# One load queue with the input first, and token-major denominators in the linear-attention layers of a four-layer kernel

## The chip, the cores and the metric

The kernel runs on one core of a Trainium2 chip. The metric is the device time of one execution in microseconds (us), as a median over several executions. A core has five engines that run side by side and wait for one another through semaphores: TensorE (PE in the profile, with its weight loads listed apart as PEld), VectorE (DVE), ScalarE (ACT), GpSimd (POOL) and SyncE (SP), which here only issues transfers. TensorE's clock is granted by a throttle; "granted clock 0.5" means half speed.

## The reference

The input is one sequence of 2048 tokens with 512 channels in bf16. Four layers follow one another, A, B, A, B. Both kinds have 32 heads of 16 channels. The two A layers share their weights, and so do the two B layers.

```python
def A(x, wqkv, wo):                  # linear attention
    q, k, v = split(x @ wqkv)        # each (32 heads, 2048, 16)
    phi = lambda t: where(t > 0, t + 1, exp(t)) + 1e-6
    pq, pk = phi(q), phi(k)
    kv  = einsum("bhsd,bhse->bhde", pk, v)
    z   = einsum("bhsd->bhd", pk)
    num = einsum("bhqd,bhde->bhqe", pq, kv)
    den = einsum("bhqd,bhd->bhq", pq, z)[..., None] + 1e-6
    return merge(num / den) @ wo

def B(x, wqkv, wo): ...              # softmax attention, sliding window of 256

x = x + A(layernorm(x), A_wqkv, A_wo)
x = x + B(layernorm(x), B_wqkv, B_wo)
x = x + A(layernorm(x), A_wqkv, A_wo)
x = x + B(layernorm(x), B_wqkv, B_wo)
```

What matters here is that `den` is one number for each token and head: 2048 x 32 numbers, a sixteenth of `num`.

## The kernel before

The kernel is a chain of stages: setup, and then for each layer the projection to q, k and v (qkv), the attention, and the output projection. Each stage is a block with one instruction list for each engine, and at the end of a block all engines meet. Time saved by one engine in a stage therefore counts only if that engine was what the stage's end waited for.

**Setup.** Three engines issue loads, each on its own queue. GpSimd builds constants, VectorE builds masks out of them and only then takes the statistics of x. ScalarE makes the layernorm's factor (`rstd`) as exp(-0.5 ln(var + eps)).

```python
# SyncE                               # T = 16 tiles of 128 tokens
for gi in range(4):
    load(xres[:, 4 tiles of group gi], x)        # 512 KB each
load(wA_o); load(wB_o)
# ScalarE
load(wA_qkv)                                     # 1536 KB
wait(statistics); ln_rstd = Exp(-0.5 * Ln(var + eps))
# GpSimd
load(wB_nat)                                     # 1536 KB
memset(...); iota(...)
g.drain()
affine_select(ident ...); affine_select(maskLo ...); affine_select(maskHi ...)
signal(constants)
# VectorE
wait(constants)
... masks out of the constants ...
for gi in range(4):
    wait(x group gi)
    for t in group gi: bn_stats(ln_stats[:, t], xres[:, t])
for t in range(T): bn_aggr(ln_mv[:, t], ln_stats[:, t])
signal(statistics)
```

**A-attention.** Numerator and denominator are both made channel-major, that is, with channels on the partitions and tokens along the free dimension. The denominator is made as a full 128x512 tile, in which each of a head's 16 partitions holds the same number. `KV8` is the K-V product masked to blocks of 16x16, and `Z8` is z spread over the same blocks. The division is a Ln and an Exp on ScalarE and a multiply on VectorE. TensorE's results go to PSUM tensors; a slot is a part of one, which the kernel lets TensorE overwrite only after it has been read.

```python
# TensorE
for f in range(4): pkv[f] = sum over 16 tiles of pk[t].T @ vA[t]   # 64 matmuls
for u in range(16):                       # u = (f, c): 128 channels, 512 tokens
    if u >= 2: wait(Ln u - 2)             # two PSUM slots
    pe.matmul(pden[:, u % 2, :], Z8[:, f, :], pqT[:, f, c])        # 128x512
for u in range(16):
    if u >= 2: wait(multiply u - 2)       # two PSUM slots
    pe.matmul(pnum[:, u % 2, :], KV8[:, f, :], pqT[:, f, c])
# ScalarE
for u in range(16): d2[:, u] = Ln(pden[:, u % 2] + 1e-6)
a.drain()
for u in range(16): d2[:, u] = Exp(-d2[:, u])
# VectorE
for u in range(16):
    wait(Exp u); wait(matmul u)
    v.tensor_tensor(oT[:, f, c], pnum[:, u % 2, :], d2[:, u, :], mult)
```

**Output projection.** For A, `oT` is channel-major already and is used as it is. For B, the result is token-major, and each tile takes four transposes on TensorE and a copy on ScalarE first:

```python
def emit_matmuls(pe, t):
    for f in range(4):
        lhsT = oTt[:, t % 2, f, :] if from_tok else oT[:, f, tile t]
        pe.matmul(pwo[:, t % 4, :], lhsT, w_o[:, f, :], start=(f == 0), stop=(f == 3))
```

VectorE then adds the residual and takes the next layernorm's statistics.

The softmax here doesn't subtract the row's maximum and nothing guards it: scores larger than these inputs give would overflow.

## Time and profile before

The time is 866.53 us, the median of 4 runs (865.32 to 867.28). I cut the profiled execution (865.6 us) into stages, each from the first TensorE matmul of a stage to the first of the next:

| stage | us |
|---|---|
| setup | 29.50 |
| layer 1 (A): qkv, attention, projection | 66.76, 29.56, 27.30 |
| layer 2 (B) | 297.32 |
| layer 3 (A): qkv, attention, projection | 65.75, 30.43, 26.91 |
| layer 4 (B) | 292.07 |

The B layers are two thirds of the time, and the change doesn't touch them. It touches setup, the two A-attentions and the two A-projections.

The following lines are from the timeline of the kernel before, in setup. The columns are start in us, duration in us, engine, source line, operation, output and input, shapes, count; in brackets stands how long the engine had been idle and what released it.

```profile
13.62 0.29 POOL L200 TENSOR_SCALAR_AFFINE_SELECT ident<-ident 128x128 bf16<-128x128 bf16 x1 [10.30 <-issue]
14.54 0.15 DVE L219 TENSOR_SCALAR itmp_m<-itmp_p 128x1 int32<-128x1 int32 x1 [14.54 <-POOLq L213]
15.78 9.59 DVE L231 BATCH_NORM_STATS2 ln_stats<-xres 128x6 f32<-128x512 bf16 x16
25.44 1.17 DVE L234 BATCH_NORM_AGGREGATE ln_mv<-ln_stats 128x2 f32<-128x6 f32 x16
26.67 0.31 ACT L151 ACTIVATE ln_rstd<-ln_mv,epsln 128x16 f32<-128x16 f32 x1 [24.05 <-DVEq L235]
27.03 1.28 ACT L153 ACT_TABLE_LOAD   x1
29.50 1.01 PE L329 MATMUL pst<-ident,xn 128*128 128x128 bf16 x8 [29.50 <-DVE xn L427]
```

It is a serial chain. GpSimd stands idle for 10.30 us and goes on at 13.62; VectorE starts its masks at 14.54, its statistics at 15.78; ScalarE follows at 26.67, and TensorE gets its first work at 29.50. The next lines are the page's list of DMA issues of the kernel before: output and input, queue, count, KB each, and the median us from issue to landing.

```profile
xres<-in_A_x_dram SPq DMA_DIRECT2D x4, 512.0 KB, 13.5
wA_qkv<-in_A_wqkv_dram ACTq DMA_DIRECT2D x1, 1536.0 KB, 12.3
wB_nat<-in_B_wqkv_dram POOLq DMA_DIRECT2D x1, 1536.0 KB, 12.1
```

The three queues carry data at the same time. Both weights have landed by 13.4 us (0.80 + 12.3 = 13.1 for A, 1.32 + 12.1 = 13.4 for B), but of the input, which is needed first, only one quarter: its four landings are recorded at 8.55, 14.33, 15.85 and 17.35 us. GpSimd's own load landed at 13.4 us, just ahead of the end of GpSimd's idle time.

The timeline of the kernel before, in the first A-attention, with the same columns:

```profile
101.92 9.90 ACT L572 ACTIVATE d<-pden,eps 128x512 f32<-128x512 f32 x16 [4.43 <-remote]
111.90 1.28 ACT L575 ACT_TABLE_LOAD   x1
113.19 9.90 ACT L575 ACTIVATE d<-d,zero 128x512 f32<-128x512 f32 x16
113.94 1.30 DVE L562 TENSOR_TENSOR oT<-pnum,d 128x512 bf16<-128x512 f32 x2 [11.52 <-ACT d L575]
115.41 1.30 DVE L562 TENSOR_TENSOR oT<-pnum,d 128x512 bf16<-128x512 f32 x2 [0.16 <-PE pnum L533]
```

ScalarE works for 9.90 + 1.28 + 9.90 = 21.1 us. VectorE can't start its multiplies before the first Exp, so it waits 11.52 us; from then on two multiplies take 1.47 us (113.94 to 115.41), with a short wait for TensorE after each pair. The same stage in the view by groups (line, engine, operation, names, shapes, count; busy us, mean ns of one; idle us before it and its releasers), and the view by windows of the multiply loop (window, its length, then busy us and instruction count of PE, PEld, DVE, ACT and POOL, granted clock, DMA share, GB/s):

```profile
L562 DVE TENSOR_TENSOR oT<-pnum,d 128x512 bf16<-128x512 f32 x16 | 10.4, 691 | 12.7 <-ACT d L575 11.7 <-PE pnum L533 1.0
```

```profile
114.00:125.50 11.50, 8.51 (x14) 1.47 (x14) 10.35 (x16) 9.10 (x15) 0.00 (x0) 0.50 0.00 0
```

The loop ran at a granted clock of 0.50, with VectorE busy for 10.35 of 11.50 us.

### The profile page before, as it was taken

How to read it: one execution, taken by the hardware profiler on the slowest of the kernel's cores; microseconds unless marked ns; L12 is line 12 of the kernel's file. 1: busy time of each engine (PE TensorE's matmuls, PEld its weight loads, DVE VectorE, ACT ScalarE, POOL GpSimd, SP SyncE). 2: the span in 40 equal slices, each digit the busy share in tenths (PEclk: the TensorE clock that was granted, in tenths of full speed). 3: DMA queues.
4: the chain of work that ended last, by engine and by line, in shares of the span. 5: the costliest groups of instructions: out<-in, count | busy, mean ns of one | idle time of the engine just before them, and what ended most of it. 6: DMA issues, size and time to landing. Idle time of an engine off the chain costs nothing. (4 is left out here: it accounts for less than half of the span.)

```text
span 865.6 us, 16040 instructions
## 1 busy us (share of the span) xinstructions
PE 678.7 (78%) x5478; PEld 316.6 (37%) x5504; DVE 594.0 (69%) x2750; ACT 632.4 (73%) x884; POOL 5.7 (1%) x22
## 2 busy tenths in 40 slices
PE   0578675798888888888867887848978888888888
PEld 0333412443343343434433342323433434333344
DVE  3577658434777878777685783854378787887875
ACT  0577670456999999999656778134589999999984
POOL 1000000000000000000000000000000000000000
PEclk9999958799555555555688996769965555555559
DMA  8000000000000000000000000000000000000002
GB/s 291 0 1 1 1 0 0 2 1 1 1 2 2 1 2 1 2 1 2 2 1 1 1 1 0 1 0 1 1 1 2 2 2 2 1 2 2 2 2 98
DMA packets 6353, 9.41 MB, mean 11 GB/s; under 512 B 384, under 2 KB 5504, under 8 KB 6272
## 3 DMA queue, kind: packets, MB, share of 16 engines
q1 hardware_dynamic: 5472, 5.24, 1.9%
q10 hardware_dynamic: 528, 1.57, 0.5%
q0 software_dynamic: 272, 1.57, 0.5%
q8 instruction: 44, 0.72, 0.3%
q14 instruction: 37, 0.30, 0.1%
HBM read 6.29 MB, written 2.10 MB: 10 GB/s over the span
## 5 line engine op out<-in xcount | busy, mean ns | idle before, releaser
L786 ACT ACTIVATE PTs<-st,zero 128x768 bf16<-128x768 f32 (+2 forms) x512 | 404.8, 859 | 22.0 <-PE st L741 10.2
L823 DVE TENSOR_TENSOR PTs<-PTs,maskHi 128x128 bf16<-128x128 bf16 x1024 | 220.2, 221 | 79.2 <-ACT PTs L786 78.2
L760 PE MATMUL U<-vB,PTs 128*128 128x17 bf16 x2880 | 163.1, 179 | 67.3 <-DVE PTs L827 62.6
L760 PEld LDWEIGHTS U<-vB,PTs 128*128 128x128 bf16 x2880 | 116.2, 106 | 244.4 <-DVE PTs L827 228.4
L827 DVE TENSOR_TENSOR PTs<-PTs,maskLo 128x128 bf16<-128x128 bf16 x896 | 196.2, 219 | 0.0
L741 PE MATMUL st<-qT,kT 16*128 16x384 bf16 (+2 forms) x512 | 121.5, 472 | 2.2 <-PEq L311 2.2
L741 PE MATMUL st<-qT,kTB 32*128 32x384 bf16 (+2 forms) x512 | 122.5, 474 | 0.0
L329 PE MATMUL pst<-ident,xn 128*128 128x128 bf16 x256 | 30.0, 270 | 82.4 <-DVE xn L427 78.2
L367 PE MATMUL pss<-wA_qkv,xnT 128*128 128x512 bf16 x255 | 64.0, 395 | 0.3 <-issue 0.2
L367 PE MATMUL pss<-xnT,wB_qk 128*128 128x512 bf16 x248 | 61.5, 391 | 0.8 <-ACT xnT L389 0.4
L656 DVE TENSOR_TENSOR xres<-pwo,xres 128x512 bf16<-128x512 f32 x64 | 43.5, 680 | 21.6 <-PE pwo L621 21.6
L389 ACT ACTIVATE xnT<-pst 128x512 bf16<-128x512 bf16 x64 | 34.9, 595 | 30.1 <-PE pst L329 29.6
L242 ACT ACTIVATE tmpE<-pss,zero 128x512 f32<-128x512 f32 x64 | 44.0, 688 | 17.5 <-PE pss L367 11.0
L461 DVE TENSOR_SCALAR kTB<-kT,maskB 128x512 bf16<-128x512 bf16 x32 | 11.3, 353 | 64.9 <-ACT kT L408 64.9
L151 ACT ACTIVATE ln_rstd<-ln_mv,epsln 128x16 f32<-128x16 f32 x4 | 1.2, 308 | 73.5 <-DVEq L666 49.4
L329 PEld LDWEIGHTS pst<-ident,xn 128*128 128x128 bf16 x256 | 19.6, 116 | 95.4 <-DVE xn L427 51.6
L246 DVE TENSOR_SCALAR tmpE<-tmpE 128x512 f32<-128x512 f32 x64 | 27.0, 422 | 25.6 <-ACT tmpR L243 25.3
L803 DVE TENSOR_TENSOR o_tok<-U,densb 128x128 bf16<-128x128 f32 x128 | 37.4, 292 | 9.6
L243 ACT ACTIVATE tmpR<-pss,zero 128x512 bf16<-128x512 f32 x64 | 43.9, 686 | 0.0
L408 ACT ACTIVATE qT<-pss 128x512 bf16<-128x512 f32 x32 | 19.1, 597 | 32.7 <-PE pss L367 32.7
L367 PEld LDWEIGHTS pss<-wA_qkv,xnT 128*128 128x128 bf16 x256 | 26.3, 103 | 34.7 <-issue 7.9
L562 DVE TENSOR_TENSOR oT<-pnum,d 128x512 bf16<-128x512 f32 x32 | 20.9, 690 | 26.2 <-ACT d L575 24.0
(69 smaller groups left out, 648.6 us busy)
## 6 DMA issues: line engine op xcount, KB each, us to landing
xres<-in_A_x_dram SPq DMA_DIRECT2D x4, 512.0 KB, 13.5
out_dram<-xres SPq DMA_DIRECT2D x16, 128.0 KB, 1.7
wA_qkv<-in_A_wqkv_dram ACTq DMA_DIRECT2D x1, 1536.0 KB, 12.3
wB_nat<-in_B_wqkv_dram POOLq DMA_DIRECT2D x1, 1536.0 KB, 12.1
wA_o<-in_A_wo_dram SPq DMA_DIRECT2D x1, 512.0 KB, 13.8
wB_o<-in_B_wo_dram SPq DMA_DIRECT2D x1, 512.0 KB, 9.4
```

The source lines that it names most:

```text
L242: a.activation(self.tmpE[:, js, :], ps_ap, ACT.Exp, bias=z)
L243: return a.activation(self.tmpR[:, js, :], ps_ap, ACT.Relu, bias=z)
L329: mm = pe.transpose(pst[sl2][:, kt, :], self.xn[:, sl2, kt * P : (kt + 1) * P], self.ident[:])
L367: mm = pe.matmul(pss[:, sl, :], lhsT, rhs, start=(kt == 0), stop=(kt == 3))
L389: s_cp.inc(a.activation(self.xnT[:, :, t * P : (t + 1) * P], pst[sl2][:], ACT.Copy))
L656: s_res.inc(v.tensor_tensor(self.xres[:, t, :], pwo[:, sl, :], self.xres[:, t, :], ALU.add))
L741: mm = pe.matmul(ST[sl][:, e, 0:n], lhsT, rhs, start=True, stop=True, tile_position=(32 * (hs % 4), 0))
L760: mm = pe.matmul(ut[:, hs, 0:17], lhsT, rhs, start=(ci == 0), stop=(ci == len(cl) - 1))
L786: a.activation(self.PTs[:, j % NJS, hp[0] : hp[0] + 2, 0:n], ST[sl][:, :, 0:n], ACT.Exp, bias=self.zero1[:], scale=DH ** -0.5,)
L803: v.tensor_tensor(self.o_tok[:, jd, fd * P : (fd + 1) * P].rearrange("p (h d) -> p h d", d=DH), ut[:, :, 0:DH], dsb.to_broadcast([P, 8, DH ...
L823: op = v.tensor_tensor(self.PTs[:, js, hs, 0:P], self.PTs[:, js, hs, 0:P], self.maskHi[:], ALU.mult)
L827: op = v.tensor_tensor(self.PTs[:, js, hs, 2 * P : 3 * P], self.PTs[:, js, hs, 2 * P : 3 * P], self.maskLo[:], ALU.mult,)
```

## The change

The intent has two parts. In setup, all loads go onto SyncE's queue with x in front, and the statistics come ahead of the masks, so that VectorE starts as soon as x is there. In A-attention, the denominator is made token-major, that is, with tokens on the partitions, as 32 numbers for each token rather than 512. Its reciprocal then costs a sixteenth of the elements, and the multiply reads it broadcast over the 16 channels of a head. The price is that the result is token-major, so A's projection needs the transposes that B's has.

```diff
 # setup, SyncE
   for gi in range(NG): load(xres group gi)
+  s_wA.inc(e.dma_start(self.wA_qkv[:], ...), 16)
+  s_wB.inc(e.dma_start(self.wB_nat[:], ...), 16)
   load(wA_o); load(wB_o)
 # setup, ScalarE
-  s_wA.inc(a.dma_start(self.wA_qkv[:], ...), 16)
 # setup, GpSimd
-  s_wB.inc(g.dma_start(self.wB_nat[:], ...), 16)
 # setup, VectorE
+  for gi in range(NG): wait(x group gi); bn_stats of its four tiles
+  bn_aggr of 16 tiles
+  v.wait_ge(s_c.h, s_c.v(1)); s_stat.inc(v.nop())
   v.wait_ge(s_c.h, s_c.v(1))
   ... masks, and bm8 [P, 8] ...
-  bn_stats and bn_aggr as above
@@ A-attention @@
 # TensorE
-  16 x pe.matmul(pden[:, sl, :], self.Z8[:, f, :], pqT of 512 tokens)
-  16 x pe.matmul(pnum[:, sl, :], self.KV8[:, f, :], pqT of 512 tokens)
+  for t in range(T):
+      for f in range(4):
+          pe.matmul((pdA if t < KD else pdB)[:, t, f * 8 : (f + 1) * 8],
+                    self.pqT[:, f, t * P : (t + 1) * P], self.Zs[:, f, :])
+  for t in range(T):
+      if t >= 2: pe.wait_ge(s_od.h, s_od.v(t - 1))
+      for f in range(4):
+          pe.matmul(pnum[:, t % 2, f * P : (f + 1) * P],
+                    self.pqT[:, f, t * P : (t + 1) * P], self.KV8[:, f, :])
 # VectorE                                                  KD = 4
-  16 x v.tensor_tensor(oT[...], pnum[:, sl, :], self.d2[:, u, :], ALU.mult)
+  for t in range(KD): v.reciprocal(self.den_all[:, t, :], pdA[:, t, :])
+  for t in range(T):
+      if t == KD: v.wait_ge(s_r.h, s_r.v(1))
+      v.tensor_tensor(o_tok[:, t, :], pnum[:, t % 2, :],
+                      self.den_all[:, t, :].unsqueeze(2).to_broadcast([P, H, DH]), ALU.mult)
 # ScalarE
-  16 x Ln of 128x512, then 16 x Exp of 128x512
+  a.activation(rest, pdB[:, KD:T, :], ACT.Ln, bias=self.eps6[:])        # 128x384
+  s_r.inc(a.activation(rest, rest, ACT.Exp, bias=self.zero1[:], scale=-1.0))
@@ A's projection @@
-  self.phase_wo(self.wA_o, last=last, first=(li == 0), from_tok=False)
+  self.phase_wo(self.wA_o, last=last, first=(li == 0), from_tok=True)
```

Buffers, PSUM tiles and semaphores that follow from this are cut. VectorE's reciprocals leave out the 1e-6 that the Ln adds as its bias.

More of the change, by code (lines that the diff above doesn't have):

```diff
@@ L91, in run @@
             self.blockmask = self.sb("blockmask", [P, P], dt.float32)
+            self.bm8 = self.sb("bm8", [P, 8], dt.float32)
             self.maskLo = self.sb("maskLo", [P, P], dt.bfloat16)
@@ L102, in run @@
             self.itmp_t = self.sb("itmp_t", [P, P], dt.int32)
+            self.itmp_t8 = self.sb("itmp_t8", [P, 8], dt.int32)
+            self.itmp_m8 = self.sb("itmp_m8", [P, 8], dt.int32)
             self.ln_stats = self.sb("ln_stats", [P, T, 6], dt.float32)
@@ L115, in run @@
                         self.vA = self.lsb(lctx, "vA", [P, T, 4, 132], dt.bfloat16)
-                        self.oT = self.lsb(lctx, "oT", [P, 4, self.S], dt.bfloat16)
+                        self.o_tok = self.lsb(lctx, "o_tokA", [P, T, D], dt.bfloat16)
+                        self.oTt = self.lsb(lctx, "oTtA", [P, 2, 4, P], dt.bfloat16)
                         self.KV8 = self.lsb(lctx, "KV8", [P, 4, P], dt.bfloat16)
-                        self.Z8 = self.lsb(lctx, "Z8", [P, 4, P], dt.bfloat16)
+                        self.Zs = self.lsb(lctx, "Zs", [P, 4, 8], dt.bfloat16)
                         self.zc = self.lsb(lctx, "zc", [P, 4], dt.float32)
@@ L121, in run @@
                         self.tmpR = self.lsb(lctx, "tmpR", [P, 2, 512], dt.bfloat16)
-                        self.d2 = self.lsb(lctx, "d2", [P, 4 * C, 512], dt.float32)
+                        self.den_all = self.lsb(lctx, "den_all", [P, T, H], dt.float32)
                         self.phase_qkv("A", first=(li == 0))
                         self.phase_attn_A(first=(li == 0))
-                        self.phase_wo(self.wA_o, last=last, first=(li == 0), from_tok=False)
+                        self.phase_wo(self.wA_o, last=last, first=(li == 0), from_tok=True)
                 else:
@@ L177, in _ @@
                     s_xg[gi].inc(e.dma_start(self.xres[:, gi * tg : (gi + 1) * tg, :], xv[:, gi * tg : (gi + 1) * tg, :]), 16)
+                s_wA.inc(e.dma_start(self.wA_qkv[:], self.A_wqkv.rearrange("(kt p) c -> p kt c", p=P)), 16)
+                s_wB.inc(e.dma_start(self.wB_nat[:], self.B_wqkv.rearrange("(kt p) c -> p kt c", p=P)), 16)
                 s_wAo.inc(e.dma_start(self.wA_o[:], self.A_wo.rearrange("(kt p) c -> p kt c", p=P)), 16)
@@ L182, in _ @@
             def _(a):
-                s_wA.inc(a.dma_start(self.wA_qkv[:], self.A_wqkv.rearrange("(kt p) c -> p kt c", p=P)), 16)
                 a.wait_ge(s_stat.h, s_stat.v(1))
@@ L188, in _ @@
             def _(g):
-                s_wB.inc(g.dma_start(self.wB_nat[:], self.B_wqkv.rearrange("(kt p) c -> p kt c", p=P)), 16)
                 g.memset(self.ident[:], 0.0)
@@ L198, in _ @@
                 g.iota(self.itmp_t[:], pattern=[[1, P]], base=0, channel_multiplier=0)
+                g.iota(self.itmp_t8[:], pattern=[[1, 8]], base=0, channel_multiplier=0)
                 g.drain()
@@ L217, in _ @@
             def _(v):
+                for gi in range(NG):
+                    v.wait_ge(s_xg[gi].h, s_xg[gi].v16(1))
+                    for t in range(gi * tg, (gi + 1) * tg):
+                        v.bn_stats(self.ln_stats[:, t, :], self.xres[:, t, :])
+                v.drain()
+                for t in range(T):
+                    v.bn_aggr(self.ln_mv[:, t, :], self.ln_stats[:, t, :])
+                v.drain()
+                v.wait_ge(s_c.h, s_c.v(1))
+                s_stat.inc(v.nop())
                 v.wait_ge(s_c.h, s_c.v(1))
@@ L226, in _ @@
                 v.drain()
-                s_c.inc(v.tensor_single_scalar(self.blockmask[:], self.itmp_m2[:], 0.0, ALU.is_equal), 1)
-                for gi in range(NG):
-                    v.wait_ge(s_xg[gi].h, s_xg[gi].v16(1))
-                    for t in range(gi * tg, (gi + 1) * tg):
-                        v.bn_stats(self.ln_stats[:, t, :], self.xres[:, t, :])
+                v.tensor_single_scalar(self.blockmask[:], self.itmp_m2[:], 0.0, ALU.is_equal)
+                v.tensor_tensor(self.itmp_m8[:], self.itmp_p[:, 0:8], self.itmp_t8[:], ALU.subtract)
                 v.drain()
-                for t in range(T):
-                    v.bn_aggr(self.ln_mv[:, t, :], self.ln_stats[:, t, :])
-                v.drain()
-                s_stat.inc(v.nop())
+                s_c.inc(v.tensor_single_scalar(self.bm8[:], self.itmp_m8[:], 0.0, ALU.is_equal), 1)
         self.commit_all()
@@ L488, in phase_attn_A @@
         s_kvz = self.sem("kvz")
-        s_nd = self.sem("nd")
-        s_ln2 = self.sem("lnden")
-        s_d2 = self.sem("d2")
+        s_den = self.sem("den")
+        s_dcp = self.sem("dcp")
+        s_r = self.sem("rall")
+        s_num = self.sem("num")
         s_od = self.sem("odone")
-        s_num = self.sem("num")
         s_wB = self.sem("ld_wB")
         s_pm = self.sem("permB")
-        NU = 4 * C
         with (
@@ L499, in phase_attn_A @@
             nc.psum_tensor(self.uname("pnum"), [P, 2, 512], dt.float32) as pnum,
-            nc.psum_tensor(self.uname("pden"), [P, 2, 512], dt.float32) as pden,
+            nc.psum_tensor(self.uname("pden"), [P, 16, H], dt.float32) as pdA,
+            nc.psum_tensor(self.uname("pden"), [P, 16, H], dt.float32) as pdB,
             nc.Block() as blk,
         ):
+            KD = 4
             @blk.tensor
@@ L516, in _ @@
                     s_kv.inc(mm)
-                for f in range(4):
-                    pe.wait_ge(s_kvz.h, s_kvz.v(f + 1))
-                    for c in range(C):
-                        u = f * C + c
-                        sl = u % 2
-                        if u >= 2:
-                            pe.wait_ge(s_ln2.h, s_ln2.v(u - 1))
-                        rhs = self.pqT[:, f, c * 512 : (c + 1) * 512]
-                        s_nd.inc(pe.matmul(pden[:, sl, :], self.Z8[:, f, :], rhs, start=True, stop=True))
-                for f in range(4):
-                    for c in range(C):
-                        u = f * C + c
-                        sl = u % 2
-                        if u >= 2:
-                            pe.wait_ge(s_od.h, s_od.v(u - 1))
-                        rhs = self.pqT[:, f, c * 512 : (c + 1) * 512]
-                        s_num.inc(pe.matmul(pnum[:, sl, :], self.KV8[:, f, :], rhs, start=True, stop=True))
+                pe.wait_ge(s_kvz.h, s_kvz.v(4))
+                for t in range(T):
+                    sl = t % 2
+                    mm = None
+                    for f in range(4):
+                        mm = pe.matmul(
+                            (pdA if t < KD else pdB)[:, t, f * 8 : (f + 1) * 8],
+                            self.pqT[:, f, t * P : (t + 1) * P],
+                            self.Zs[:, f, :],
+                            start=True,
+                            stop=True,
+                        )
+                    s_den.inc(mm)
+                for t in range(T):
+                    sl = t % 2
+                    if t >= 2:
+                        pe.wait_ge(s_od.h, s_od.v(t - 1))
+                    mm = None
+                    for f in range(4):
+                        mm = pe.matmul(
+                            pnum[:, sl, f * P : (f + 1) * P],
+                            self.pqT[:, f, t * P : (t + 1) * P],
+                            self.KV8[:, f, :],
+                            start=True,
+                            stop=True,
+                        )
+                    s_num.inc(mm)
             @blk.vector
@@ L538, in _ @@
                     v.wait_ge(s_wB.h, s_wB.emitted)
-                    last = None
+                    lastop = None
                     for qk in range(2):
@@ L545, in _ @@
                                 i_ap = self.wB_nat[:, kt, c0 : c0 + 128].rearrange("p (eh el d) -> p el eh d", eh=2, el=4, d=DH)
-                                last = v.tensor_copy(o_ap, i_ap)
-                    s_pm.inc(last)
+                                lastop = v.tensor_copy(o_ap, i_ap)
+                    s_pm.inc(lastop)
                 for f in range(4):
@@ L552, in _ @@
                     v.drain()
-                    s_kvz.inc(
-                        v.tensor_scalar(self.Z8[:, f, :], self.blockmask[:], self.zc[:, f : f + 1], None, op0=ALU.mult)
-                    )
-                for u in range(NU):
-                    f, c = u // C, u % C
-                    sl = u % 2
-                    v.wait_ge(s_d2.h, s_d2.v(u + 1))
-                    v.wait_ge(s_num.h, s_num.v(u + 1))
+                    s_kvz.inc(v.tensor_scalar(self.Zs[:, f, :], self.bm8[:], self.zc[:, f : f + 1], None, op0=ALU.mult))
+                v.wait_ge(s_den.h, s_den.v(KD))
+                for t in range(KD):
+                    v.reciprocal(self.den_all[:, t, :], pdA[:, t, :])
+                v.drain()
+                for t in range(T):
+                    sl = t % 2
+                    if t == KD:
+                        v.wait_ge(s_r.h, s_r.v(1))
+                    v.wait_ge(s_num.h, s_num.v(t + 1))
                     s_od.inc(
                         v.tensor_tensor(
-                            self.oT[:, f, c * 512 : (c + 1) * 512], pnum[:, sl, :], self.d2[:, u, :], ALU.mult
+                            self.o_tok[:, t, :].rearrange("p (h e) -> p h e", e=DH),
+                            pnum[:, sl, :].rearrange("p (h e) -> p h e", e=DH),
+                            self.den_all[:, t, :].unsqueeze(2).to_broadcast([P, H, DH]),
+                            ALU.mult,
                         )
@@ L568, in _ @@
             def _(a):
-                for u in range(NU):
-                    sl = u % 2
-                    a.wait_ge(s_nd.h, s_nd.v(u + 1))
-                    s_ln2.inc(a.activation(self.d2[:, u, :], pden[:, sl, :], ACT.Ln, bias=self.eps6[:]))
+                rest = self.den_all[:, KD:T, :]
+                a.wait_ge(s_den.h, s_den.v(T))
+                a.activation(rest, pdB[:, KD:T, :], ACT.Ln, bias=self.eps6[:])
                 a.drain()
-                for u in range(NU):
-                    s_d2.inc(a.activation(self.d2[:, u, :], self.d2[:, u, :], ACT.Exp, bias=self.zero1[:], scale=-1.0))
+                s_r.inc(a.activation(rest, rest, ACT.Exp, bias=self.zero1[:], scale=-1.0))
         self.commit_all()
```

## The prediction

> **What bounds the kernel now.** Busy time per stretch shows four layers: two linear-attention (A), two sliding-window (B). In B (210 to 422, 632 to 847 us) ScalarE is 96% busy, untouched by the change. It touches three serial stretches:
>
> - Setup. The timeline puts the first matrix work (transposes) at 29.5 us. VectorE starts at 14.54 us, released by GpSimd, idle until 13.62 us (its own load lands 12.1 us after issue). Then masks 1.2 us, sixteen bn_stats 9.6 us, aggregation 1.2 us, ScalarE's rstd with a 1.28 us table load 1.95 us.
> - A-attention, 96.2 to 125.5 us, and 516.2 to 546.2 us. K-V product 5.4 us; then 16 Ln of a 128x512 denominator 9.9 us, a table load 1.28 us, 16 Exp 9.9 us; VectorE's 16 multiplies start behind the first Exp, 0.73 us each, alternating with two PSUM slots at a granted clock of 0.5.
> - A output projection: 21.8 us from first matmul to last bn_stats, paced by VectorE at 1.19 us a tile.
>
> **What changes.**
>
> *Setup.* All loads go onto one queue, x first; bn_stats precede the masks. The Trainium skill, "DMA: Bandwidth & Descriptors", Queues, rings and completion order, says each DMA engine round-robins between queues with work; the trace agrees: three queues moved about 400 GB/s together and x landed a median 13.5 us after issue. Alone, at 350 GB/s or better (the single-queue end of the load, 14 to 18 us), the first 512 KB should land at about 5 us and the rest ahead of VectorE. bn_stats run 5 to 14.7, aggregation to 15.9, rstd to 18; masks hide behind ScalarE. First transposes about 18.5 us: 10.8 us saved, all critical. Weights A land at 12 to 14 us, no wait.
>
> *A-attention.* The denominator becomes token-major, 32 columns per tile. 32 large Ln/Exp become one Ln and one Exp of 128x384 (0.58 us each, estimated between 128x256 at 0.47 and 128x512 at 0.69) plus a 1.28 us table load; four tiles go to VectorE reciprocals (0.2 us each). TensorE gets 64 matmuls of 8 columns (estimated from B's 17-column ones: 43 ns apart, 2.8 us) and 64 of 128 columns instead of 16+16 of 512. VectorE's first multiply starts about 9.4 us after the stage begins instead of 17.7. Its multiplies stay 128x512, 0.61 to 0.73 us each. Stage 20.6 instead of 29.3 us: 8.7 saved per layer. The Ln/Exp tail is ready after about 12 us, as tile 4 is reached.
>
> *Projection.* It gains transposes and a ScalarE copy per tile, as B's projection has: 23.1 us there against 21.5 to 21.8. Pace stays 1.19 us; start-up costs 1.3 us per layer.
>
> **Sum:** 10.8 + 2 x 8.7 - 2 x 1.3 = 25.6 us. Predicted 841 us, 8-in-10 range 834 to 849. Faster by over 2%: 0.91; within 2%: 0.08; slower: 0.01.
>
> **What would show it.** Right: transposes start near 18.5 us; A-attention lasts 19 to 21.5 us; multiplies 0.6 to 0.73 us apart; ScalarE's work there falls from about 21 to about 2.5 us; A projection 22.5 to 23.5 us; B layers unchanged within 1 us.
>
> **What would make it wrong.** x landing late, or SyncE blocked issuing eight transfers past 18 us (one issue took 5.8 us before), holding the stage-end barrier; 8-column matmuls costing far more than 43 ns; VectorE waiting at tile 4 for ScalarE; TensorE's clock falling to half sooner and stretching the multiply loop (or staying full and shortening it by 2 us a layer); another clock in B.

## The result and the profile after

The time after is 834.41 us, the median of 8 runs (833.66 to 836.03), against 865.98 us for the kernel before in the same rounds (13 runs, 865.01 to 867.28). All outputs are right. The ratio is 0.9637, with a 95% interval of 0.9628 to 0.9647. Here and below a ratio is the mean time of one kernel's fast runs over that of the other's of the same rounds, so it is not quite the ratio of the medians. The stages of the two profiled executions, whose spans are 865.6 and 833.2 us (known to 0.1 us, which the last two rows carry):

| stage | before | after | difference | predicted |
|---|---|---|---|---|
| setup | 29.50 | 18.71 | -10.79 | -10.8 |
| A-attention, layers 1 and 3 | 29.56, 30.43 | 19.38, 19.39 | -21.22 | -17.4 |
| A-projection, layers 1 and 3 | 27.30, 26.91 | 28.42, 28.30 | +2.51 | +2.6 |
| A-qkv, layers 1 and 3 (not changed) | 66.76, 65.75 | 65.51, 65.29 | -1.71 | 0 |
| both B layers (not changed) | 297.32, 292.07 | 296.55, 291.65 | -1.19 | 0 |
| sum | | | -32.4 | -25.6 |

Two rows match. The attention saved 3.8 us more than predicted, and the stages that the change leaves alone 2.9 us. Together they are, but for rounding and 0.1 us of the projection, the 6.8 us between -25.6 and -32.4. The profiled execution of the kernel before took 867.28 us, the slowest of the 13; by the medians the saving is 31.6 us, and the difference is in no single stage.

The timeline of the kernel after, in setup, followed by its DMA issues (columns as above):

```profile
2.19 0.29 POOL L205 TENSOR_SCALAR_AFFINE_SELECT ident<-ident 128x128 bf16<-128x128 bf16 x1 [0.20 <-issue]
4.91 9.59 DVE L226 BATCH_NORM_STATS2 ln_stats<-xres 128x6 f32<-128x512 bf16 x16 [4.91 <-DMA xres<-in_A_x_dram]
14.58 1.17 DVE L229 BATCH_NORM_AGGREGATE ln_mv<-ln_stats 128x2 f32<-128x6 f32 x16
15.88 0.31 ACT L155 ACTIVATE ln_rstd<-ln_mv,epsln 128x16 f32<-128x16 f32 x1 [13.80 <-DVEq L232]
16.23 1.28 ACT L157 ACT_TABLE_LOAD   x1
17.53 0.31 ACT L157 ACTIVATE ln_rstd<-ln_rstd,zero 128x16 f32<-128x16 f32 x1
18.71 1.01 PE L338 MATMUL pst<-ident,xn 128*128 128x128 bf16 x8 [18.71 <-DVE xn L436]
```

```profile
xres<-in_A_x_dram SPq DMA_DIRECT2D x4, 512.0 KB, 5.6
wA_qkv<-in_A_wqkv_dram SPq DMA_DIRECT2D x1, 1536.0 KB, 10.4
wB_nat<-in_B_wqkv_dram SPq DMA_DIRECT2D x1, 1536.0 KB, 13.5
```

The statistics start at 4.91 instead of 15.78 us, released by the input's landing, and then run through without a gap. Everything behind them has moved forward by the same 10.8 us. The transfer rate is not what changed: the engines moved 393 GB/s from 4 to 14 us before, and 378 GB/s from 3 to 13 us after. What changed is the order in which the data arrives, and that GpSimd is not held up. GpSimd, which issues no load now, is idle for 0.20 instead of 10.30 us. The A weights, issued at 2.92 us, landed at 2.92 + 10.4 = 13.3 us, ahead of their use.

The timeline of the kernel after, in the first A-attention:

```profile
90.39 1.66 PEld L532 LDWEIGHTS pden<-Zs,pqT 128*128 128x128 bf16 x64 [0.93 <-DVE Zs L573]
90.99 0.99 DVE L576 RECIPROCAL den_all<-pden 128x32 f32<-128x32 f32 x4 [0.65 <-PE pden L532]
92.19 0.58 ACT L596 ACTIVATE den_all<-pden,eps 128x384 f32<-128x384 f32 x1 [6.73 <-PE pden L532]
92.43 10.85 DVE L584 TENSOR_TENSOR o_tokA<-pnum,den_all 128x512 bf16<-128x512 f32 x16 [0.45 <-PE pnum L546]
92.83 1.28 ACT L598 ACT_TABLE_LOAD   x1
94.12 0.61 ACT L598 ACTIVATE den_all<-den_all,zero 128x384 f32<-128x384 f32 x1
```

The stage starts at 84.22 and ends at 103.60. The multiplies start 92.43 - 84.22 = 8.21 us into it, where before they started 113.94 - 96.26 = 17.68 us into it. ScalarE's work is 0.58 + 1.28 + 0.61 = 2.5 us, and its Exp ends at 94.73, which is when VectorE reaches tile 4 (92.43 + 4 x 0.60 = 94.83). The loop itself is hardly shorter. The groups of that stage, and the windows of the denominators' matmuls and of the later part of the loop:

```profile
L584 DVE TENSOR_TENSOR o_tokA<-pnum,den_all 128x512 bf16<-128x512 f32 x16 | 10.2, 687 | 1.1 <-PE pnum L546 0.5
L576 DVE RECIPROCAL den_all<-pden 128x32 f32<-128x32 f32 x4 | 1.0, 311 | 0.6 <-PE pden L532 0.6
```

```profile
90.40:92.00 1.60, 1.60 (x64) 1.60 (x65) 0.99 (x4) 0.00 (x0) 0.00 (x0) 1.00 0.00 0
...
95.00:103.00 8.00, 6.62 (x44) 3.74 (x44) 7.47 (x12) 0.00 (x0) 0.00 (x0) 0.50 0.00 0
```

A multiply with a broadcast operand takes 687 ns where one with a full operand took 691, so the broadcast costs nothing here. The denominators' matmuls ran at a clock of 1.00; in the loop the clock falls to 0.50, as it did before.

### The profile page after: what moved, and what is told of

Its sections match the earlier page's. It is cut to its first block, busy times and chain, and to the rows that moved or that the text cites. A ratio compares the mean times of both kernels' runs of the same rounds, so it can differ in the third digit from the quotient of the medians.

```text
span 833.2 us, 16681 instructions
## 1 busy us (share of the span) xinstructions
PE 669.1 (80%) x5796; PEld 331.5 (40%) x5824; DVE 594.7 (71%) x2760; ACT 613.5 (74%) x856; POOL 4.8 (1%) x22
## 5 line engine op out<-in xcount | busy, mean ns | idle before, releaser
L809 ACT ACTIVATE PTs<-st,zero 128x768 bf16<-128x768 f32 (+2 forms) x512 | 404.9, 860 | 22.5 <-PE st L764 10.9
L679 DVE TENSOR_TENSOR xres<-pwo,xres 128x512 bf16<-128x512 f32 x64 | 43.6, 681 | 23.5 <-PE pwo L644 23.5
L669 ACT ACTIVATE oTtA<-pstwo 128x512 bf16<-128x512 bf16 x32 | 18.9, 597 | 36.6 <-PE pstwo L629 36.6
L376 PEld LDWEIGHTS pss<-xnT,wB_qk 128*128 128x128 bf16 x256 | 25.4, 100 | 30.2 <-issue 2.6
## 6 DMA issues: line engine op xcount, KB each, us to landing
wA_qkv<-in_A_wqkv_dram SPq DMA_DIRECT2D x1, 1536.0 KB, 10.4
```

Source lines behind the costliest of these rows:

```text
L376: mm = pe.matmul(pss[:, sl, :], lhsT, rhs, start=(kt == 0), stop=(kt == 3))
L679: s_res.inc(v.tensor_tensor(self.xres[:, t, :], pwo[:, sl, :], self.xres[:, t, :], ALU.add))
L809: a.activation(self.PTs[:, j % NJS, hp[0] : hp[0] + 2, 0:n], ST[sl][:, :, 0:n], ACT.Exp, bias=self.zero1[:], scale=DH ** -0.5,)
```

## The experiments

Twelve kernels ran, in three calls of four; the kernels of a call share a chip and the runs of the kernel before. The kernel before had medians of 865.4, 865.92 and 865.37 us in the three calls.

### Call 1: which half gives what

**setup_only** is the kernel before with the changed setup alone.

```diff
 # kernel before
-  wA_qkv on ScalarE's queue, wB_nat on GpSimd's; masks, then statistics
+  both on SyncE's queue behind x; statistics, then masks
```

> The kernel before with only the changed setup (loads on one queue, x first, statistics before masks). Theory 'the parts add': about 855.2 us (866.0 - 10.8), first transposes at about 18.7 us, A-attention stages still 29.5 to 30.4 us. Rival 'the setup gain is partly given back later' (weights land later on one queue and a later stage waits for them): 857 to 860 us and a wait of TensorE for the A weights after the transposes.

It took 854.45 us, ratio 0.9873 (0.9854 to 0.9892). Setup lasted 18.62 us; the A-attentions (29.99 and 30.06) and projections (27.00, 26.91) stayed as before. The gain is 10.95 us, the same as the 10.88 us by which the stage is shorter: nothing of it was given back later.

**attn_only** is the other half.

```diff
 # kernel after
-  wA_qkv, wB_nat on SyncE's queue; statistics, then masks
+  wA_qkv on ScalarE's queue, wB_nat on GpSimd's; masks, then statistics
```

> The changed kernel with the old setup. Theory 'the parts add': the two A layers give 21.2 us (10.2 + 11.0) and lose 2.5 us in the projections, so about 847 us, first transposes at 29.5 us. Rival 'the attention gain needs the new setup': clearly above 849 us.

It took 848.37 us, ratio 0.9795 (0.978 to 0.9809), with A-attentions of 19.37 and 19.38 us, projections of 28.41 and 28.33, and setup at 29.81 us. The gain is 17.03 us.

**queue_only** keeps the single queue and puts the masks first again.

```diff
 # kernel after, setup, VectorE
-  statistics of x; wait(constants); masks
+  wait(constants); masks; statistics of x
```

> The changed kernel with the masks before the statistics again, all loads still on one queue. Theory 'the queue is what pays, the reorder is free': VectorE is idle until x lands at 4.9 us and the constants are ready at about 3 us, so the 1.65 us of masks fit in front; time equal to the changed kernel within 0.5 us (834.4). Rival 'the reorder pays too': 1 to 1.7 us slower.

It took 835.95 us, ratio 0.965 (0.9634 to 0.9667), with setup at 18.51 us. That is 0.6 us above after_again of the same call, with intervals that overlap, and setup is no longer. The order on VectorE is worth nothing once the queues are as in the kernel after: the masks run from 3.11 to 4.75 us, and the input lands just then (statistics start at 4.79).

**after_again** is the kernel after, unchanged, to stand beside these.

> The changed kernel once more, for a second profile. The first profile has 1.25 us less than the kernel before between the first transposes and the first K-V product (65.5 against 66.8 us), in code that the change does not touch. Theory 'the clock phase of that one execution': here the stretch comes out differently, anywhere in 65.0 to 67 us, and the cold-to-full-speed switch (7.5 us after the first transposes in the first profile) moves with it. Rival 'the change causes it': 65.5 us again, switch at 7.5 us.

It took 835.37 us, ratio 0.9646 (0.9632 to 0.9661). The two halves sum to 10.95 + 17.03 = 27.98 us, and the whole gained 30.03 us. The 2 us between are not resolved: the product of the two ratios is 0.9671, against 0.9646, each with an interval of about 0.0015 to 0.002 to either side. In the profiles the touched stages add up: 10.9 us shorter in setup_only and 18.7 in attn_only make 29.6, against 29.5 in the kernel after. I found no interplay of the two halves.

### Call 2: inside each half

**reorder_only** asks what the order alone would have given.

```diff
 # kernel after, setup
-  SyncE: x, wA_qkv, wB_nat, wA_o, wB_o
+  SyncE: x, wA_o, wB_o;  ScalarE: wA_qkv;  GpSimd: wB_nat
```

> The changed kernel with the loads back on three queues (A weights on ScalarE's, B weights on GpSimd's), statistics still before masks. Theory 'the queue is what pays': x shares the DMA engines with 3 MB of weights again, statistics start at 8 to 12 us and starve until the last x lands at 16 to 18 us, first transposes at 23 to 25 us instead of 18.7, time 839 to 841 us. Rival 'the reorder is what pays': first transposes near 19 us, time 834 to 836 us.

It took 841.77 us, ratio 0.9722 (0.9708 to 0.9737), and setup lasted 25.82 us, a little beyond the 23 to 25 us expected: 3.7 of the 10.8 us. Its timeline in setup:

```profile
9.07 2.47 DVE L226 BATCH_NORM_STATS2 ln_stats<-xres 128x6 f32<-128x512 bf16 x4 [9.07 <-DMA xres<-in_A_x_dram]
13.68 0.29 POOL L205 TENSOR_SCALAR_AFFINE_SELECT ident<-ident 128x128 bf16<-128x128 bf16 x1 [10.26 <-issue]
14.40 7.22 DVE L226 BATCH_NORM_STATS2 ln_stats<-xres 128x6 f32<-128x512 bf16 x12 [2.86 <-DMA xres<-in_A_x_dram]
```

With three queues the first quarter of x is there at 9.07 instead of 4.91 us, and the second only at 14.40, after VectorE had starved for 2.86 us. This is what sharing the DMA engines costs the transfer that is needed first. The Trainium skill, "DMA: Bandwidth & Descriptors", Queues, rings and completion order, says that each DMA engine takes turns between the queues that have work; the trace agrees in kind. GpSimd again stands idle for 10.26 us, as before, and 0.20 us without a load of its own. In both runs it goes on about 0.2 us after its own load has landed. I infer that its drain waits for that landing. No run takes the drain away, so that reading is argued, not shown.

**all_scalar** and **all_vector** ask whether splitting the reciprocals between two engines matters.

```diff
 # all_scalar: kernel after, A-attention
-  KD = 4
+  KD = 0           # no reciprocal on VectorE; Ln and Exp of 128x512
 # all_vector: kernel after, A-attention
-  KD = 4; four reciprocals of 128x32; Ln and Exp of 128x384
+  KD = T; v.reciprocal(self.den_all[:], pdA[:])     # one of 128x512; ScalarE idle
```

> The changed kernel with no VectorE reciprocals: all 16 tiles' denominators by ScalarE's Ln and Exp. Theory 'four reciprocals hide ScalarE's 2.5 us chain (Ln, table load, Exp)': the first multiply waits for the end of Exp, about 2.3 us later than now, stage about 21.7 us instead of 19.4, time about 839 us. Rival 'the chain was not on the path': within 0.5 us of 834.4 to 835.4.

> The changed kernel with no ScalarE in the denominator: one VectorE reciprocal of 128x512. Theory 'reciprocal costs by element' (128x8 took 201 ns, 128x32 took 311 ns, so about 4.6 ns per element): about 2.5 us for it, first multiply about 2.4 us later, time about 839 to 840 us. Rival 'a VectorE operation of this size costs 0.7 us like the others': first multiply 0.5 us later, time about 836 us.

They took 841.95 us (ratio 0.9729, 0.9709 to 0.9748) and 842.31 us (0.9728, 0.9712 to 0.9745). The A-attentions lasted 22.11 and 22.12 us in all_scalar, 22.76 and 22.73 in all_vector, against 19.4. Both times lie above the 839 and 839 to 840 us expected, 7.5 and 7.9 us above the 834.41 of the kernel after. The two attention stages account for 5.5 and 6.7 us of that; the kernel after did not run in this call, so the rest is not resolved. First the multiplies of all_scalar in its first A-attention, then the reciprocal and the multiplies of all_vector there (timelines):

```profile
94.71 11.04 DVE L580 TENSOR_TENSOR o_tokA<-pnum,den_all 128x512 bf16<-128x512 f32 x16 [4.64 <-ACT den_all L594]
```

```profile
92.16 3.36 DVE L575 RECIPROCAL den_all<-pden 128x512 f32<-128x512 f32 x1 [1.85 <-PE pden L532]
95.59 11.05 DVE L581 TENSOR_TENSOR o_tokA<-pnum,den_all 128x512 bf16<-128x512 f32 x16
```

With ScalarE alone, VectorE waits 4.64 us for Ln, table load and Exp; alone on VectorE, a reciprocal of 128x512 takes 3.36 us. In the kernel after, four small reciprocals (0.99 us, under the tail of the denominators' matmuls) carry VectorE over ScalarE's whole chain. The split is worth about 2.7 us a layer against ScalarE alone, and 3.4 against VectorE alone. The reciprocal was sized too low: 128x32 takes 311 ns and 128x512 takes 3358, so between these two sizes an element along the free dimension costs (3358 - 311) / 480 = 6.3 ns. From 128x8 (201 ns, in B) to 128x32 it is (311 - 201) / 24 = 4.6 ns, so the one small step did not foretell the large size.

**slots4** asks what paces the multiply loop once the clock has fallen: VectorE itself, or the wait for a free PSUM slot. It gives the numerators four slots. The two extra ones lie in banks that the K-V product has left by then.

```diff
 # kernel after, A-attention
-  slot = pnum[:, t % 2];          if t >= 2: wait(multiply t - 2)
+  slot = pnum[:, t % 4] if t % 4 < 2 else pkv[:, t % 4 - 2];  if t >= 4: wait(multiply t - 4)
```

> The changed kernel with four PSUM slots for the numerator instead of two (two of the K-V banks are reused). In the changed kernel the multiplies are 0.60 us apart for five tiles at full clock and 0.70 us apart after the clock falls to half. Theory 'at half clock the two-slot round trip to TensorE binds': all 16 multiplies 0.60 us apart, loop 9.7 instead of 10.9 us, stage about 18.2 us, time about 832 us (2.3 us less than the changed kernel). Rival 'VectorE itself is slower there': no change.

It took 833.84 us, ratio 0.9637 (0.9617 to 0.9657), no different from the kernel after; about 832 was expected. Yet the stage fell to 17.98 and 18.18 us, 1.4 and 1.2 us less. In the first of these two stages the clock stayed full nearly to the end, so only the second tests the loop at half clock. The timeline of slots4 near the end of its second A-attention:

```profile
506.66 1.21 PE L551 MATMUL pnum<-KV,pqT 128*128 128x128 bf16 x8 [0.20 <-DVE o_tokA L589]
507.12 1.28 DVE L589 TENSOR_TENSOR o_tokA<-pkv,den_all 128x512 bf16<-128x512 f32 x2
508.31 1.28 DVE L589 TENSOR_TENSOR o_tokA<-pnum,den_all 128x512 bf16<-128x512 f32 x2
```

Here the matmuls are slow already (eight in 1.21 us), and the multiplies still come 0.60 us apart (507.12 to 508.31 for two), without a wait. In the kernel after, with two slots, they are 0.70 us apart at that clock. So at half clock the slots were the limit, and not VectorE. But the projection that follows took 28.78 and 28.80 us instead of 28.42 and 28.30.

### Call 3: given back, or lost in the spread

**after_third** and **slots4_again** are the kernel after and slots4 once more, unchanged, beside each other. Either the gain of slots4 is real and lost in the spread of single executions, or the next stage gives it back.

> The changed kernel a third time, as the reference of this call and for a third profile of the same program: 834 to 836 us; the stretch from first transposes to K-V product again 65.0 to 67 us, following the time of the clock switch.

> Four PSUM slots once more, beside the changed kernel on the same chip: its profile had the two A-attention stages 1.4 and 1.2 us shorter but the projections after them 0.4 and 0.5 us longer. Theory 'a net 1.5 to 2 us remains': 1.0 to 2.5 us below the changed kernel of this call. Rival 'given back in the projection': no difference.

They took 833.9 us (ratio 0.9631, 0.9614 to 0.9648) and 835.5 us (0.9641, 0.9621 to 0.9662). The attention stage of slots4 is again 1.0 and 1.2 us shorter (18.19 and 18.17 against 19.20 and 19.39), and the projection again longer (28.94 and 28.80 against 28.23 and 28.29). The loads of TensorE's weights at the start of the projection show why. First the kernel after, then slots4_again (timelines of the first A-projection):

```profile
107.84 0.15 PEld L644 LDWEIGHTS pwo<-wA_o,oTtA 128*128 128x128 bf16 x1 [0.28 <-issue]
108.22 0.43 PEld L629 LDWEIGHTS pstwo<-ident,o_tokA 128*128 128x128 bf16 x4 [0.23 <-issue]
```

```profile
108.14 0.36 PEld L634 LDWEIGHTS pstwo<-ident,o_tokA 128*128 128x128 bf16 x3 [0.28 <-issue]
108.95 0.32 PEld L649 LDWEIGHTS pwo<-wA_o,oTtA 128*128 128x128 bf16 x2 [0.22 <-issue]
```

Lone loads with 0.28 us of idle time before them, about 0.43 us apart, are TensorE at half speed; closely packed groups are full speed. The granted clock says the same: it reads 0.50 from 103.60 to 108.20 us in the kernel after and from 103.05 to 108.90 in slots4_again, and 1.00 behind. The kernel after is at full speed 4.6 us after its first transposes (108.22 after 103.57), slots4_again only 5.9 us after them (108.95 after 103.02). The third layer repeats it: 517.84 after 513.22, and 518.60 after 512.73. So part of what a shorter loop saves is taken by a longer cold start of the projection: 0.5 to 0.7 us of some 1.1. Another part goes in the stage after that, the q, k and v stage of the B layer. It took 55.32 and 55.35 us in slots4_again (55.24 and 55.35 in slots4) against 54.87 and 54.99 in after_third, with the clock at half for 7.6 us at its start instead of 6.7 and 6.9. Of the two layers' gain, 0.2 of 2.2 us is then left for slots4_again against after_third, and 1.1 of 2.6 for slots4 against the kernel after. That is no more than the spread of the other stages. The q, k and v stage of the first layer, for one, took 66.32 us in this execution and 65.14 in after_third.

**sqrt_rstd** takes a table load out of each layernorm by making `rstd` with a square root on ScalarE and a reciprocal on VectorE.

```diff
 # kernel after
-  ScalarE: ln_rstd = Exp(-0.5 * Ln(var + eps))
+  ScalarE: ln_rstd = Sqrt(var + eps)
 # qkv stage, VectorE
+  v.reciprocal(ln_rstd, ln_rstd); v.drain()
```

> The changed kernel with 1/sqrt(var) as one ScalarE Sqrt and one VectorE reciprocal in place of Ln, table load, Exp. Theory 'the rstd chain is on the path of all four layers': each loses a 1.28 us table load and one 0.31 us activation and gains a reciprocal of 128x16 of about 0.3 us, so 1.2 to 1.4 us per layer, about 5 us in all, 829 to 831 us. Rival 'given back': the Exp table has to be loaded in the next stage instead, and the gain is under 1.5 us.

It took 835.98 us, ratio 0.9653 (0.9634 to 0.9673): no gain. The A-projections, in which `rstd` is made, fell to 26.90 and 26.77 us, 1.3 and 1.5 less than in after_third. But the stages behind them grew: qkv of the first layer took 67.17 us (65.14 in after_third), qkv of the third 66.78 (65.27), and qkv of each B layer 0.9 more. Setup stayed at 18.75 us, because the masks on VectorE hold the stage's end until 17.5 us anyway. The timeline of ScalarE in sqrt_rstd shows where the loads went:

```profile
24.57 1.28 ACT L249 ACT_TABLE_LOAD   x1
25.86 0.69 ACT L249 ACTIVATE tmpE<-pss,zero 128x512 f32<-128x512 f32 x1
187.98 1.28 ACT L809 ACT_TABLE_LOAD   x1 [1.27 <-PEq L318]
```

The table for Exp is now loaded in front of the first Exp of a later stage, instead of at the end of the stage that makes `rstd`. The load wasn't removed, only moved.

**best** joins queue_only's setup, slots4 and sqrt_rstd, so that the masks no longer hold setup.

```diff
 # kernel after
+  queue_only's order in setup, slots4's four slots, sqrt_rstd's square root
```

> Masks in front, four PSUM slots and the Sqrt form together on top of the changed kernel. If the parts add: 5 + 1.5 us below the changed kernel, 827 to 829 us; the setup gains nothing by itself from masks in front. Rival 'they share a wait': above 830 us.

It took 832.33 us where 827 to 829 was expected, ratio 0.9614 (0.9594 to 0.9634), with setup at 17.20 and the A-attentions at 18.16 and 18.19 us. That is 1.6 us under after_third, with intervals that overlap. It may be a little faster than the kernel after; these runs don't separate them.

## Why the prediction was right, and where a size was off

**The total.** 841 us was predicted with a range of 834 to 849; 834.41 was measured, at its very edge, and the two repeats took 835.37 and 833.90 us. That the range held was partly luck. The mechanism held in every stage that the change touches. The saving was 25.6 us in the prediction and 31.6 by the medians (32.4 by the two profiled spans).

**Setup: right.** "First transposes about 18.5 us: 10.8 us saved, all critical": they came at 18.71, and the stage saved 10.79 us. Each step was seen: statistics from 4.91 to 14.5 us, `rstd` ready at 17.84 (17.53 + 0.31), weights at 13.3 us, before their use. What the prediction didn't say is which part does it. queue_only shows that the single queue alone gives all of it, and reorder_only that the order alone gives 3.7 us. The single queue does two things, though: x lands earlier, and GpSimd, without a load of its own, is not held up. In reorder_only the statistics don't wait for GpSimd, so the 7.1 us that it lacks are the input's late landing; no run frees GpSimd and leaves three queues. SyncE had issued its last load by 9.5 us, so the feared block of its queue didn't come.

**A-attention: right in kind, 3.8 us too small in size.** Two terms were mis-sized.

- "43 ns apart, 2.8 us" for the 64 matmuls of the denominators. They took 1.66 us, 26 ns apart. B's matmuls, from which the 43 ns came, are hardly further apart. The second of these lines of the timeline of the kernel before has 12 weight loads in 0.51 us, 43 ns for each; but these are two groups of six, with 0.14 us from the last start of the one (421.28) to the first start of the other (421.42), and the length of the last load is counted too. The first line has one group of six.

```profile
299.94 0.24 PEld L760 LDWEIGHTS U<-vB,PTs 128*128 128x128 bf16 x6 [0.66 <-DVE PTs L827]
421.14 0.51 PEld L760 LDWEIGHTS U<-vB,PTs 128*128 128x128 bf16 x12 [0.52 <-DVE PTs L823]
```

  A load lasts 0.10 us, so six of them are (0.24 - 0.10) / 5 = 28 ns apart, at a granted clock of 0.50 and with 17 columns. So it was the wait in the 43 ns, and not the clock. The Trainium skill, "TensorE: Matmul & The Clock Gate", section Wait — 56ns, not 53.3ns?, says that the distance from start to start never falls below about 25 ns; the 26 ns here agree. This term is most of "first multiply starts about 9.4 us after the stage begins", which measured 8.21: 2 x 1.2 us. What follows the first multiply was right: 20.6 - 9.4 = 11.2 us predicted, 19.38 - 8.21 = 11.17 measured. Of that the multiply loop is 10.85: the first five multiplies were 0.60 us apart at full clock, the others 0.70.
- "Instead of 29.3 us" for the stage before. It is 29.56 in the first A layer and 30.43 in the second, where sixteen Ln took 10.40 instead of 9.90 us. I had costed both layers from a rounded reading of the first: 0.26 + 1.13 = 1.4 us.

Together: 2 x (20.6 - 19.4) + 1.4 = 3.8 us. One term went the other way. "Reciprocals (0.2 us each)" measured 311 ns; it cost nothing, since VectorE was waiting for the first numerator anyway (0.45 us before 92.43).

**Tile 4: right, with luck.** ScalarE's Exp ended at 94.73, tile 4 was due at 94.83. That is 10.5 us into the stage, where 12 was predicted; both sides of the race came earlier, and 0.1 us was left. all_scalar and all_vector show that the split between the engines is needed; without it the stage is 2.7 or 3.4 us longer.

**Projection: right.** "Start-up costs 1.3 us per layer"; 1.12 and 1.39 were measured. From first matmul to last `bn_stats` the projection took 23.6 us in both layers (103.60 to 127.19 in the first), at the upper edge of the 22.5 to 23.5 forecast.

**Untouched stages: predicted 0, measured -2.9 us.** 1.25 us of it is the first layer's qkv stage. The timelines of the weight loads in that stage, first the kernel before, then the kernel after:

```profile
38.30 0.35 PEld L367 LDWEIGHTS pss<-wA_qkv,xnT 128*128 128x128 bf16 x2 [0.28 <-issue]
38.77 0.75 PEld L367 LDWEIGHTS pss<-xnT,wA_qkv 128*128 128x128 bf16 x4
```

```profile
25.80 0.15 PEld L376 LDWEIGHTS pss<-wA_qkv,xnT 128*128 128x128 bf16 x1 [0.28 <-issue]
26.23 0.97 PEld L376 LDWEIGHTS pss<-wA_qkv,xnT 128*128 128x128 bf16 x5 [0.28 <-issue]
```

Before, the last load with the slow spacing came at 38.30 us, 8.8 us after the first transposes (29.47); after, at 26.23 us, 7.55 us after them (18.68). The difference is the stage's difference. The trace's first entry for the granted clock, at full speed, stands at 38.36 us before and at 26.23 after. But it changes from one execution to the next of the same program: three profiled executions of the kernel after had 7.55, 7.99 and 6.67 us, and stages of 65.51, 65.92 and 65.14 us; two of slots4 had 6.69 and 8.40 us, and 65.18 and 66.32 us. So one pair of profiles can't put this difference down to the change. It can't rule the change out either: the two executions with the old setup (66.76 us, and 66.58 in attn_only) took longer than all ten with another setup and the old `rstd` (65.14 to 66.32). The Trainium skill, "TensorE: Matmul & The Clock Gate", Part 1: The HAM clock gate, gives a reason: TensorE gets its full clock after a busy window of about 3.4 us, and the windows run freely, so the switch falls at another place each time. The trace agrees in kind: the switch came 6.7 to 8.8 us after the first, sparse transposes, and its place varied. Of the other 1.65 us, 0.9 lie in the q, k and v stages of the B layers: 55.57 and 55.30 us before, 54.95 and 54.99 after. The clock stayed at half for their first 8.1 and 7.6 us before, and for 6.9 us after. setup_only, with the old attention, has 55.25 and 55.49 us there, and all three executions of the kernel after have 54.9 to 55.0. So this piece seems to come with the change, through a shorter cold start; no run takes it apart. The rest stays open.

## What to carry to other kernels

Put the load that the first work needs alone at the front, and count the queues that move data beside it: here one queue gave 10.8 us, and the order of the instructions nothing on top. A value that is the same for 16 channels should be inverted once and broadcast in the multiply, and a short chain on one engine can be hidden by giving a second engine just enough of the work to last until it is done. After cutting a stage, look at the next one, since a slower start of TensorE's clock or a table load that only moved can take the gain back, and before using a distance between instructions from another stage, take out the waits in it and the length of the last one.

## What the Trainium skill lacked or had wrong

- "VectorE: DVE Perf Modes", First, the fixed hardware budget, says that Reciprocal is an iterative divide with a repeat count of 8, but gives no cost. Measured: 311 ns for 128x32 and 3358 ns for 128x512 in float32 from PSUM, 6.3 ns for each further element along the free dimension; 128x8 took 201 ns. A multiply of 128x512 takes 687 ns.
- "ScalarE: Activation LUTs", What ACT_TABLE_LOAD costs, gives 1283 ns for the load and about 1380 ns of drain, 2.66 us for a switch. The load agrees (1283 ns). The drain wasn't seen: Ln ended at 16.19 us, the load ran from 16.23, and Exp started at 17.53, so a switch cost 1.34 us.
- The same page, Table sets: the hidden batching unit, says that Ln and then Exp need one load. The compiled program loads a table between Ln and Exp each time (at 27.03 and 111.90 us before, at 16.23 and 92.83 after). The page doesn't say when the compiler picks the joint set.
- "TensorE: Matmul & The Clock Gate", Back-to-back issue gap, gives sustained distances of about 131 ns for 512 columns and 81 ns for 128. At a clock of 1.00, four of 512 columns took 1.03 us, the last of them 0.38, so 0.22 us apart, and of the numerators' matmuls of 128 columns four took 0.40 and eight 0.61 us, so (0.61 - 0.40) / 4 = 0.05 us apart. These are near the page's figures for an isolated matmul; nothing here showed 131 ns.
- No page that I found says that GpSimd's next work after its own load's issue and a drain can stand until that load has landed: 10.30 and 10.26 us of idle time with the load, 0.20 us without it, and it went on about 0.2 us after the landing. That the drain is the cause is inferred.
- "TensorE: Matmul & The Clock Gate", Part 1, warns that the clock-gate events of a trace can be unreliable. No page that I found says that they can be missing before the first switch, so that a view reads 1.00 there while TensorE is still at half speed. The window from 18.70 to 26.20 us of the kernel after reads 1.00, yet weight loads of 512-column matmuls are 0.43 us apart in it, and 0.22 later; the first entry for the clock stands at 26.23 us. The spacing is what to go by there.
